# Hash attention and maxout feed-forward on one core: weight and load order, DMA transposes of x, and V sums on Pool

## The chip, the cores and the metric

The kernel runs on one core of a Trainium2 chip. The metric is the device time of one execution in microseconds (us). Five runs of the kernel before took 276.6 to 278.73 us, median 277.15.

Five engines work side by side, each through its own instructions in a fixed order: PE (TensorE: matmuls, and transposes as matmuls with an identity), ACT (ScalarE), DVE (VectorE), POOL (GpSimd) and SP (SyncE, which here issues DMAs). POOL also issues DMAs, in a queue of its own. An instruction that waits holds up all that stand behind it on its engine.

## The reference

```
q_bits = (q @ proj > 0);  k_bits = (k @ proj > 0)      # 6 bits per row
bucket = sum(bits * 2**i)
mask   = q_bucket[:, None] == k_bucket[None, :]
scores = where(mask, q @ k.T / sqrt(64), -1e9)
attn   = exp(scores - max);  attn = attn / (sum(attn) + 1e-9)
x      = (attn @ v), heads side by side                 # 3072 x 512
h      = maximum(maximum(x @ w1, x @ w2), x @ w3)       # 3072 x 768
out    = h @ w_out                                      # 3072 x 512
```

There are 4 batches of 8 heads, 768 rows each, 64 columns a head. Inputs and output are float32; the matrix products run in float16 pieces.

## The kernel before

**Attention.** Heads are worked in pairs, so a batch has pairs 0 to 3, written (b, pr). For each pair q and k are loaded (`load`, L236) and split into a float16 value and its remainder (`split_h` L252/L254, `split_r` L259, tile `s`), then transposed to `T`: in batches 0 and 1 by PE (`pe_T` L278, tile `tps`) and an evacuation on DVE or ACT, in batches 2 and 3 by a DMA transpose on SP (L268). `hash_mm` (L295, L297) multiplies `T` by the projections; DVE turns signs into bits, PE transposes these (`bit_T` L324), and they go to DRAM and back (`bit_out` L334 as `dr<-bt`, `bit_in` L337 as `T<-dr`), since they must lie in other partitions of `T`: these are the hash rows. With them one score matmul gives product and bucket match together. For pair (0, 0) the rows come by PE instead.

A *unit* is one head's 384 query rows against 256 keys: two score matmuls `sc` (L380), one exponential `AT` (L386, 128x768 on ACT) and six matmuls `av` (L398) with V and a column of ones. There are 192 units, in blocks of six; a block fills the only `av` bank, which `norm_t` (L415) and `norm_x` (L421, L433) empty into `xn`. A *half* (b, hf) is 384 rows of a batch with all heads. Batch 0 runs pair 0 for both halves first, then pairs 1 to 3 of half 0, then of half 1; later batches run half by half.

**Mean of V.** `norm_t` adds a tiny multiple of the column sums of V. `vcast` (L188, L190) casts V to float16 (`vone`; on POOL in batch 0, on ACT later). In batch 0 `mean_mm` (L358) sums with six matmuls a pair from `vone`; in later batches `vsum` (L348 to L351) adds the six chunks on POOL in three instructions, and `mean_mm` (L361) is one matmul. `mean_evac` (L367) takes the result `svp` to `mv`.

**Feed-forward.** Each half needs x transposed (`xT`): `x_T` (L448, tile `xps`, three PE transposes a pair) with `x_evac` for both halves of batch 0 and for the last half, `x_bar` (L441), one DMA transpose on SP, for the other five. Then come 18 groups of four `ps` matmuls (`l1`, L462) with evacuation and maximum (L471), and three groups of six `po` matmuls (`l2`, L476), copied out (`osb`) and stored (L485). The weights are loaded on POOL's queue with a cast to float16: six loads (three matrices, left and right half; L519) and `w_out` (L634). `weights` ties groups of these loads to hash rows by `hold` (L624), a tiny POOL copy that waits for the rows.

**Order.** A planner (`Plan.run`, L44) sets the order of every engine at build time. Each task has an engine or a choice of two, an assumed duration, a priority (mostly its unit number), and the buffers it takes and gives; the planner steps through assumed time and emits the ready task of lowest priority for each free engine. Transfers run in its model as rings, and `POST` is the assumed time from a transfer's end to its notice. The instructions then run in this order whatever the real times are. Loads of batch 1 and later are tied by `after` to hash rows having been issued (`g`, L544).

Of the kernel before, what the change touches and what calls it, by code (L numbers as in the profile page):

```python
# [13 lines left out]

POST = 2.0

# [10 lines left out]
class Plan:  # L27
# [16 lines left out]
    def run(self):  # L44
# [8 lines left out]
        busy = dict.fromkeys(engines, 0.0)  # L53
        rings = {e: [] for e in engines}
        now, events, n = 0.0, [], 0
        while n < len(self.tasks):
            moved = True
            while moved:
                moved = False
                for e in engines:  # L60
                    if busy[e] > now:
                        continue
                    best = None
                    for t in ready:
                        dur = dict(t.kinds).get(e)
                        if dur is None or any(self.free[r] <= 0 for r in t.take) or any(
                                x.start is None for x in t.after):
                            continue
                        if best is None or (t.prio, t.n) < (best[0].prio, best[0].n):
                            best = t, dur  # L70
                    if best is None:
                        continue
                    t, dur = best
                    ready.discard(t)
                    for r in t.take:
                        self.free[r] -= 1
                    busy[e] = now + dur
                    t.start, t.engine = now, e
                    events.append((busy[e], -1, None))
                    if t.xfer:  # L80
                        events.append((busy[e] + 0.9, -2, t))
                    else:
                        events.append((now + dur + (t.lat or self.LAT[e]), t.n, t))
                    if t.emit:
                        t.emit(e)
                    n += 1
                    moved = True
            events.sort(key=lambda x: x[:2])
            heads = [r[0] for r in rings.values() if r]
            after = min((h[0] for h in heads)) * len(heads) if heads else 1e9  # L90
            if not events and not heads:
                stuck = [(t.kinds, t.prio, [r for r in t.take if self.free[r] <= 0])
                         for t in sorted(ready, key=lambda t: t.prio)]
                raise RuntimeError(f"plan stuck: {n} of {len(self.tasks)} at {now}, {self.free}: {stuck[:12]}")
            then = min(now + after, events[0][0] if events else 1e9)
            for h in heads:
                h[0] -= (then - now) / len(heads)
            now = then
            for r in rings.values():
                while r and r[0][0] < 1e-6:  # L100
                    t = r.pop(0)[1]
                    events.append((now + POST, t.n, t))
            events.sort(key=lambda x: x[:2])
            while events and events[0][0] <= now:
                at, kind, t = events.pop(0)
                if kind == -2:
                    rings[t.engine].append([t.xfer, t])
                    continue
                if t is None:
                    continue  # L110
                for r in t.give:
                    self.free[r] += 1
                for x in users.get(t, ()):
                    left[x] -= 1
                    if not left[x]:
                        ready.add(x)
# [4 lines left out]
def kernel(  # L121
# [37 lines left out]
    HT = 13  # L159
    XN = 3  # L160
    OSB = 3
# [47 lines left out]
    PAB = konst.tile([P, 2 * NBITS], FP16, name="PAB")  # L209
    xn0 = konst.tile([P, 2, CH, P], FP16, name="xn0")  # L210
    w_sb = [konst.tile([P, NJ, DF], FP16, name=f"w{i}_sb") for i in range(3)]
# [141 lines left out]
    def mean_mm(b, pr, e):  # L353
        ps = bank(("m", b, pr), "svp")
        o = ps[:, 0 : 2 * (D + 1)].rearrange("p (h d) -> p h d", h=2)
        if b == 0:
            for c in range(NCH):
# [59 lines left out]
    def norm_x(blk, e):  # L417
# [4 lines left out]
        if items[0][0] == items[1][0]:  # L422
            hf = items[0][0]
            if (b, hf) not in xhs:
                xhs[b, hf] = xnp.tile([P, NP, CH, P], FP16, tag="xn", name="xn")
            xn = xns[b, hf, pr] = xhs[b, hf][:, pr]
            xv = xn.rearrange("p c (h d) -> p h c d", h=2)
        else:
            hh = items[0][1]
            xv = xn0[:, :, :, hh * D : (hh + 1) * D]  # L430
            for hf in range(2):
                xns[b, hf, pr] = xn0[:, hf]
        nc.vector.tensor_tensor(out=xv, in0=t[:, :, :, 0:D], in1=rr[:].to_broadcast([P, 2, CH, D]), op=AluOp.mult)  # L433
# [6 lines left out]
    def x_bar(b, hf, e):  # L440
        nc.sync.dma_start_transpose(x_tile(b, hf)[:].rearrange("p j (c t) -> p (j c) t", t=P),  # L441
                                    xhs.pop((b, hf))[:].rearrange("p j c d -> p (j c d)"))

# [81 lines left out]
    def value(b, pr, dep):  # L525
        U = first_unit[b, pr]
        prev = at_last.get((b - 2, pr))
        if b == 0:
            ready_v[b, pr] = add(("POOL", 0.85), U - 6, [dep, prev], lambda e: vcast(b, pr, e), give=("v",))
            vs = ready_v[b, pr]  # L530
        else:
            ready_v[b, pr] = add(("ACT", 0.72), U - 6, [dep, prev], lambda e: vcast(b, pr, e))
            vs = add(("POOL", 2.0), U - 5, [dep, ready_v[b, pr], ready_m.get((b if pr > 1 else b - 1, (pr + 2) % 4))],
                     lambda e: vsum(b, pr, e), give=("v",))
        m = add(("PE", 0.34 if b == 0 else 0.06), U - 3, [vs], lambda e: mean_mm(b, pr, e), take=("mm",))
        ready_m[b, pr] = add(("DVE", 0.28), U - 3, [m], lambda e: mean_evac(b, pr, e), give=("mm",))

    def prep(b, pr):
# [3 lines left out]
        if b > 0:  # L542
            for n in "qkv":
                g = {("q", 0): (0, 1), ("k", 0): (0, 2), ("v", 0): (0, 2)}.get((n, pr), (0, 3) if pr < 2 else (1, 0)  # L544
                                                                            ) if b == 1 else divmod(4 * b + pr - GATE, 4)
                loads[n, b, pr, (0, 2)] = add(("SP", 0.5), U - 44 + 0.1 * "qkv".index(n), [],
# [59 lines left out]
        if b == 0 and pr < NP - 1:  # L606
            return_later.append(pr)
            for hh in range(2):
                ready_T[b, pr, hh] = [bi]
            return  # L610
        if (b, pr) == (0, NP - 1):
            weights(0, 0, [(0, 0), (0, 1)])
            for i in return_later:
                weights(0, i, stage[0, i])
        if (b, pr) in stage:
# [10 lines left out]
    def weights(b, pr, parts):  # L626
        if pr or b:
            prev = add(("POOL", 0.1), -150, [bounced[b, pr]], lambda e: hold(b, pr, e), after=[wprev[0]])
        else:
            prev = ready_v[0, NP - 1]  # L630
        for w in parts:
            if w == "o":
                prev = add(("POOL", 0.8), -90, [],
                           lambda e: nc.gpsimd.dma_start(wout_sb[:], moe_w_out.rearrange("(c p) m -> p c m", p=P)),  # L634
                           xfer=4.2, after=[prev])
            else:
                prev = add(("POOL", 0.8), -100, [], lambda e, w=w: load_w(w[1], w[0], e), xfer=1.9, after=[prev])
            wload[w] = prev
        wprev[0] = prev

    wprev = [None]
    return_later = []
    stage = {(0, 1): [(0, 2)], (0, 2): [(1, 0)], (0, 3): [(1, 1), (1, 2)], (1, 0): ["o"]}

# [25 lines left out]
    u = 0  # L670
    done_x, starts, has_xn = {}, {}, {}
    prev_norm = None
    for blk, (b, pr, items) in enumerate(blocks):
# [16 lines left out]
        if blk == last_block[b, pr]:  # L690
            at_last[b, pr] = prev_at
        nt = add(("DVE", 0.56), u - 20, [prev_at, ready_m[b, pr]], lambda e, blk=blk: norm_t(blk, e), take=("t",), give=("av",))
        split = items[0][0] != items[1][0]
        hf = items[0][0]
        nx = add(("DVE", 0.76), u - 20, [nt], lambda e, blk=blk: norm_x(blk, e), give=("t",),
                 take=() if split or (b, hf) in has_xn else ("xn",), after=[] if split else has_xn.get((b, hf), []))
        if split and blk == 0:
            prev_norm = nx
            continue
        if not split:  # L700
            has_xn.setdefault((b, hf), [nx])
        for hf in (0, 1) if split else (hf,):
            lst = done_x.setdefault((b, hf), [])
            tk = ("xT",) if not lst else ()
            if b == 0 or (b, hf) == (B - 1, 1):
                t = add(("PE", 0.17), u, [nx, prev_norm] if split else [nx], lambda e, b=b, hf=hf, pr=pr: x_T(b, hf, pr, e),
                        take=("mm",) + tk, after=starts.get((b, hf), []))
                starts.setdefault((b, hf), [t])
                lst.append(add(both(0.36, 0.48), u - 20, [t], lambda e, b=b, hf=hf, pr=pr: x_evac(b, hf, pr, e), give=("mm",)))
                if len(lst) == NP:  # L710
                    plan.join(lst, ("xn",))
            else:
                lst.append(nx)
                if len(lst) == NP:
                    lst = [add(("SP", 1.4), u, lst, lambda e, b=b, hf=hf: x_bar(b, hf, e), xfer=2.1, take=("xT",), give=("xn",))]
                    ffn(b, hf, lst)
                continue
            if len(lst) == NP:
                ffn(b, hf, lst)
# [32 lines left out]
```

## Time and profile before

| What | Value |
|---|---|
| median of five runs | 277.15 us |
| the profiled execution | 275.96 us |
| its span, first to last instruction | 274.2 us |
| exponentials on ACT, 192 | 146.6 us busy, 813 ns each |
| `ps` on PE, 576 | 105.2 us busy |
| `sc` on PE, 384 | 94.0 us busy |
| `av` on PE, 1152 | 66.4 us busy |
| `po` on PE, 144 | 33.7 us busy |
| `xps` on PE, 36 | 3.8 us busy |
| `svp` on PE, 24 and 12 | 2.2 and 2.6 us busy |
| first score, first `ps`, last unit done | 13.3, 52.2, about 214 us |

The span of the profile is shorter than the time of that execution by what lies outside the first and last instruction. A group's busy time is the union of its instructions; [...]bars overlap and the step from start to start is shorter than the bar. Idle time in brackets in a timeline is what the engine stood before that instruction, with the one that ended it.

### The profile page before, as it was taken

Reading aid. Unit: us, or ns where it says so; the run is one execution under the profiler, and the core shown is the slowest. Engines: PE = TensorE matmul, PEld = TensorE weight load, DVE = VectorE, ACT = ScalarE, POOL = GpSimd, SP = SyncE. Lnnn points to the kernel's source line nnn. Section 1 sums busy time; section 2 is a strip of 40 time slices with the busy share of each in tenths; the row PEclk is TensorE's granted clock in tenths of the full one; section 3 lists DMA queues with packets and bytes.
Section 4 is the critical chain, followed back from the end, with each engine's and each line's share of the span. In section 5 each row is a group of like instructions: output and inputs, shape, how many; then the busy total and the mean of one; then the engine's idle time right before and its main releaser. Section 6 shows DMA issues by size and latency. Waiting matters only on the chain.

```text
span 274.2 us, 7528 instructions
## 1 busy us (share of the span) xinstructions
PE 264.1 (96%) x3086; PEld 180.8 (66%) x3086; DVE 178.6 (65%) x400; ACT 200.0 (73%) x290; POOL 39.7 (14%) x57
## 2 busy tenths in 40 slices
PE   8899888999999999999999999999999999999994
PEld 7889666777766676676666666666666556555551
DVE  4899558999997578795499834565436635345260
ACT  4797689999996889999789888999886232322322
POOL 1250314553411103330033000000000000000000
PEclk9799799999999999999999999999999999999998
DMA  6949699795569896998969622300430021020303
GB/s 200 365 132 176 152 258 146 250 224 186 183 119 256 183 285 173 228 207 188 238 203 215 131 73 93 54 2 13 47 118 0 2 77 39 24 93 0 115 2 115
DMA packets 57872, 38.16 MB, mean 139 GB/s; under 512 B 38638, under 2 KB 54766, under 8 KB 57838
## 3 DMA queue, kind: packets, MB, share of 16 engines
q1 hardware_dynamic: 53806, 34.54, 49.1%
q0 software_dynamic: 3952, 3.15, 8.0%
q8 instruction: 24, 0.39, 0.6%
q14 instruction: 10, 0.08, 0.1%
q10 hardware_dynamic: 80, 0.00, 0.0%
HBM read 25.72 MB, written 6.84 MB: 119 GB/s over the span
## 4 chain that ended last, share of the span: by engine, by line
PE 79%; DVE 8%; DMA 6%; ACT 4%; issue 1%; SPq 1%; ACTq 0%; DVEq 0%
PE ps L462 31%; PE sc L380 19%; PE po L476 11%; PE av L398 11%; DMA k<-in_k_dram 4%; PE tps L278 3%; DVE s L259 3%; PE hps L297 2%; ACT AT L386 2%; DMA dr<-bt 2%; DVE ht L471 1%; DVE T L190 1%; DVE xn L433 1%; DVE t L415 1%; ACT vone L188 0%
## 5 line engine op out<-in xcount | busy, mean ns | idle before, releaser
L386 ACT ACTIVATE AT<-sc 128x768 f16<-128x768 f32 x192 | 146.6, 813 | 14.7 <-PE sc L380 13.9
L462 PE MATMUL ps<-xT,w_sb 128*128 128x384 f16 x576 | 105.2, 326 | 0.4 <-DVE ht L471 0.2
L380 PE MATMUL sc<-T 128*128 128x384 f16 x384 | 94.0, 328 | 2.1 <-ACT AT L386 1.7
L471 DVE TENSOR_TENSOR ht<-ht,ps 128x384 f16<-128x384 f16 x96 | 53.0, 552 | 38.0 <-PE ps L462 34.4
L398 PEld LDWEIGHTS <-AT 128*128 128x128 f16 x1152 | 60.5, 98 | 23.9 <-issue 0.9
L462 PEld LDWEIGHTS <-w_sb 128*128 128x128 f16 x576 | 52.8, 98 | 30.9 <-issue 1.0
L398 PE MATMUL av<-vone,AT 128*128 128x65 f16 x1152 | 66.4, 193 | 0.0
L188 ACT CAST ht<-ps 128x384 f16<-128x384 f32 x32 | 15.3, 479 | 33.0 <-DVE ht L471 25.5
L380 PEld LDWEIGHTS <-T 128*128 128x128 f16 x384 | 30.5, 98 | 12.9 <-issue 2.8
L476 PE MATMUL po<-wout_sb,ht 128*128 128x512 f16 x144 | 33.7, 379 | 0.0
L415 DVE TENSOR_TENSOR t<-av,mv 128x390 f32<-128x390 f32 x32 | 17.9, 560 | 14.5 <-PE av L398 14.4
L188 ACT COPY osb<-po 128x512 f32<-128x512 f32 x22 | 12.9, 586 | 16.2 <-PE po L476 16.0
L348 POOL TENSOR_TENSOR vt<-v 128x384 f32<-128x384 f32 x12 | 13.8, 1153 | 70.0 <-DMA v<-in_v_dram 69.8
L476 PEld LDWEIGHTS <-ht 128*128 128x128 f16 x144 | 13.5, 98 | 14.0
L278 PE MATMUL tps<-iden,s 128*128 128x128 f16 x216 | 19.0, 240 | 2.7 <-DVE s L259 1.7
L259 DVE SCALAR_TENSOR_TENSOR s<-q,s 128x384 f16<-128x384 f32 x32 | 20.3, 651 | 1.5 <-ACT s L252 1.4
L433 DVE TENSOR_TENSOR xn<-t,rr 128x384 f16<-128x384 f32 x32 | 20.2, 631 | 1.1
L259 DVE SCALAR_TENSOR_TENSOR s<-k,s 128x384 f16<-128x384 f32 x32 | 19.0, 610 | 0.8 <-ACT s L252 0.8
L278 PEld LDWEIGHTS <-s 128*128 128x128 f16 x216 | 15.1, 108 | 4.5 <-DVE s L259 3.8
L190 DVE CAST ht<-ps 128x384 f16<-128x384 f32 x16 | 8.9, 555 | 12.5 <-PE ps L462 12.3
L190 DVE COPY T<-tps 128x768 f16<-128x768 f16 x27 | 14.7, 552 | 2.8 <-PE tps L278 2.4
L188 ACT CAST vone<-v 128x768 f16<-128x768 f32 x12 | 10.1, 838 | 0.0
(52 smaller groups left out, 145.8 us busy)
## 6 DMA issues: line engine op xcount, KB each, us to landing
v<-in_v_dram SPq DMA_DIRECT2D x16, 384.0 KB
out_dram<-osb SPq DMA_DIRECT2D x24, 256.0 KB
q<-in_q_dram SPq DMA_DIRECT2D x15, 384.0 KB
k<-in_k_dram SPq DMA_DIRECT2D x15, 384.0 KB
w_sb<-in_moe_w_dram POOLq DMA_DIRECT2D x6, 384.0 KB, 6.6
wout_sb<-in_moe_w_out_dram POOLq DMA_DIRECT2D x1, 768.0 KB, 11.5
dr<-bt SPq DMA_DIRECT2D x15, 36.0 KB
T<-dr SPq DMA_DIRECT2D x15, 36.0 KB
```

The source lines that it names most:

```text
L188: nc.scalar.copy(o, i)
L190: ENG[e].tensor_copy(o, i)
L259: nc.vector.scalar_tensor_tensor(out=s[:, a0:a1, D : 2 * D], in0=raw_view(n, b, pr, heads), scalar=QS, in1=s[:, a0:a1, 0:D], op0=AluOp.mul ...
L278: nc.tensor.transpose(p16[:, c * P : (c + 1) * P], S16[b, pr][:, a0 + c, :], iden[:])
L380: nc.tensor.matmul(sc[:, i, 0:HQ], t[:, NA2 + hh * NCH + 2 * j + i, :], t[:, hh * NCH + hf * CH : hh * NCH + (hf + 1) * CH, :], start=True ...
L386: nc.scalar.activation(AT[:], scs.pop(u)[:, :, 0:HQ], ActFn.Exp, bias=EXP_BIAS, scale=EXP_SCALE)
L398: nc.tensor.matmul(av[:, o : o + D + 1], AT[:, i, c * P : (c + 1) * P], vones[b % 2][:, 2 * pr + hh, 2 * j + i, 0 : D + 1], start=slot == ...
L415: nc.vector.tensor_tensor(out=t[:, :, :, 0 : D + 1], in0=av[:, :, :, 0 : D + 1], in1=mv, op=AluOp.add)
L433: nc.vector.tensor_tensor(out=xv, in0=t[:, :, :, 0:D], in1=rr[:].to_broadcast([P, 2, CH, D]), op=AluOp.mult)
L462: nc.tensor.matmul(ps[:, 0:HQ], w_sb[i][:, jc, fb * P : (fb + 1) * P], xTs[b, hf][:, jc, :], start=jc == 0, stop=jc == NJ - 1)
L471: nc.vector.tensor_tensor(out=ht[:], in0=ht[:], in1=ps[:, 0:HQ], op=AluOp.max)
L476: nc.tensor.matmul(ps[:], hts[b, hf, fb][:, c * P : (c + 1) * P], wout_sb[:, fb, :], start=fb == 0, stop=fb == NF - 1)
```

## The change

- Planner's model of transfers: one queue for all instead of a ring for each engine, 2.4 us from a POOL issue to the transfer and 0.3 from an SP issue (both 0.9 before), `POST` 1.2 instead of 2.0, and larger assumed transfers of weights.
- Weights: the three left halves are issued behind the cast of v(0, 1), with no tie to hash rows. `w(1,0)` follows the rows of (0, 3), `w(1,1)` and `w(1,2)` those of (1, 0), `w_out` those of (1, 1).
- Loads of batch 1: other ties to hash rows, so that q and k of (1, 0) come behind the rows of (0, 2), and v of (1, 0) and q, k, v of (1, 1) behind those of (0, 3).
- x: every half but (0, 0) goes by `x_bar`. For batch 0 both halves have their place in `xn0`; the pool `xn` has two buffers instead of three.
- V of batch 0: pairs 1 to 3 get `vsum` on POOL and one `mean_mm` matmul.

As every assumed time feeds the planner, the order of all engines moves. In the new order SP issues copies out of (0, 1) and (0, 2), copies in of both, q and k of (1, 0), then out and in of (0, 3); the remaining loads follow. POOL runs: casts of v(0,0) and v(0,1), three weight loads, sum of pair 1, casts of pairs 2 and 3, sums of pairs 2 and 3, `hold`. The first `ps` stands behind unit 36 (behind 37 before). In PE's order the means of pairs 2 and 3 stand just before `hash_mm` of (0, 3) and unit 12. The split of (1, 0) is on DVE for q and k (q on ACT before); ACT has nine T copies up to the first `ps` instead of four, and one split instead of three.

```diff
-POST = 2.0
+POST = 1.2
+PRE_DMA = {"POOL": 2.4}
...
                     if t.xfer:
-                        events.append((busy[e] + 0.9, -2, t))
+                        events.append((busy[e] + PRE_DMA.get(e, 0.3), -2, t))
...
-            heads = [r[0] for r in rings.values() if r]
-            after = min((h[0] for h in heads)) * len(heads) if heads else 1e9
...
+            then = min(now + queue[0][0] if queue else 1e9, events[0][0] if events else 1e9)
+            if queue:
+                queue[0][0] -= then - now
...
-    XN = 3
+    XN = 2
...
-    xn0 = konst.tile([P, 2, CH, P], FP16, name="xn0")
+    xn0 = konst.tile([P, 2, NP, CH, P], FP16, name="xn0")
...
-        if b == 0:
+        if (b, pr) == (0, 0):
             for c in range(NCH):
                 nc.tensor.matmul(o, ones[:], vones[0][:, 2 * pr : 2 * pr + 2, c, 0 : D + 1],
...
-                xhs[b, hf] = xnp.tile([P, NP, CH, P], FP16, tag="xn", name="xn")
+                xhs[b, hf] = xnp.tile([P, NP, CH, P], FP16, tag="xn", name="xn")[:] if b else xn0[:, hf]
...
         if b == 0:
-            ready_v[b, pr] = add(("POOL", 0.85), U - 6, [dep, prev], lambda e: vcast(b, pr, e), give=("v",))
-            vs = ready_v[b, pr]
+            ready_v[b, pr] = add(("POOL", 0.85), U - 6, [dep, prev], lambda e: vcast(b, pr, e), give=() if pr else ("v",))
+            vs = ready_v[b, pr] if pr == 0 else add(("POOL", 2.3), U - 5, [dep, ready_v[b, pr]] + (
+                [ready_m[0, 1]] if pr == 3 else []), lambda e: vsum(b, pr, e), give=("v",))
...
-                g = {("q", 0): (0, 1), ("k", 0): (0, 2), ("v", 0): (0, 2)}.get((n, pr), (0, 3) if pr < 2 else (1, 0)
-                                                                            ) if b == 1 else divmod(4 * b + pr - GATE, 4)
+                g = divmod(4 * b + pr - GATE, 4)
+                if b == 1:
+                    g = {("q", 0): (0, 2), ("k", 0): (0, 2), ("q", 2): (1, 0), ("k", 2): (1, 0), ("v", 2): (1, 0)}.get(
+                        (n, pr), (0, 3) if pr < 2 else (1, 1))
...
-            weights(0, 0, [(0, 0), (0, 1)])
-            for i in return_later:
-                weights(0, i, stage[0, i])
+            weights(0, 0, [(0, 0), (0, 1), (0, 2)])
...
-            prev = ready_v[0, NP - 1]
+            prev = ready_v[0, 1]
...
-    stage = {(0, 1): [(0, 2)], (0, 2): [(1, 0)], (0, 3): [(1, 1), (1, 2)], (1, 0): ["o"]}
+    stage = {(0, 3): [(1, 0)], (1, 0): [(1, 1), (1, 2)], (1, 1): ["o"]}
...
-            if b == 0 or (b, hf) == (B - 1, 1):
-                t = add(("PE", 0.17), u, [nx, prev_norm] if split else [nx], lambda e, b=b, hf=hf, pr=pr: x_T(b, hf, pr, e),
-                        take=("mm",) + tk, after=starts.get((b, hf), []))
+            deps = [nx, prev_norm] if split else [nx]
+            if (b, hf) == (0, 0):
+                t = add(("PE", 0.17), u, deps, lambda e, b=b, hf=hf, pr=pr: x_T(b, hf, pr, e),
+                        take=("mm",) + (() if lst else ("xT",)), after=starts.get((b, hf), []))
...
+            if pr == NP - 1:
+                if (b, hf) != (0, 0):
+                    lst = [add(("SP", 1.4), u, lst, lambda e, b=b, hf=hf: x_bar(b, hf, e), xfer=2.1, take=("xT",),
+                               give=("xn",) if b else ())]
                 ffn(b, hf, lst)
```

## The prediction

> **What bounds the kernel now.** I read the page's busy shares and slices first, then the windows view by stage, then the chain of waits, then the timeline before the first feed-forward matmul.
>
> ```profile
> PE 264.1 (96%) x3086; PEld 180.8 (66%) x3086; DVE 178.6 (65%) x400; ACT 200.0 (73%) x290; POOL 39.7 (14%) x57
> ...
> PEclk9799799999999999999999999999999999999998
> ```
>
> ```profile
> 13.30:28.00 14.70, 14.70 (x331) 13.15 (x329) 13.61 (x33) 11.71 (x16) 3.88 (x5) 1.00 0.72 158
> 28.00:52.20 24.20, 21.17 (x312) 15.98 (x309) 16.30 (x40) 21.10 (x30) 7.30 (x13) 0.93 0.86 192
> 52.20:214.00 161.80, 161.22 (x1996) 110.17 (x1994) 116.48 (x258) 141.50 (x199) 26.74 (x33) 1.00 0.66 150
> ```
>
> ```profile
> 224.99 11.70 PE ps L462 x72
> 236.69 3.88 PE po L476 x18
> ```
>
> The reader is to see: PE is busy nearly always, and from 52.2 us on without a break; the end (chain of waits) is a train of `ps` and `po` matmuls, after attention is over at 214. Feed-forward work is the filler: whatever PE doesn't do before 214 is added behind. So every us of PE work removed, and every us that PE doesn't stand still, comes off the end. The columns of the windows are length, then busy PE, PEld, DVE, ACT and POOL, then PE's clock, the DMA share and GB/s.
>
> Busy time hides standing still, because a matmul's bar (326 ns for 384 columns) is longer than the step to the next (11.70/72 = 0.162 us). So I count by start-to-start steps, read from the timeline: `ps` and `sc` 0.162, `po` 0.216, `av` 0.029, `tps`, `xps` and `bps` 0.056, `hps` 0.025, `svp` 0.058, the opening `wps` 0.107. Times the counts: 93.3+62.2+31.1+33.4+12.1+2.0+1.7+12.0+2.1+3.4 = 253.3 us of PE work. PE's first start is 1.1, its end 270.5, and evacuation and store of the last tile take 3.7. So 16 us of the 270.5 are waits (half-clock time among them). Where? Up to the first `ps` at 52.24 the counts give 39.8 us of work, so 12.5 us of waits; after it 213.6 us of work and 4.6 of waits.
>
> ```profile
> 24.10 0.40 SPq L236 DMA_DIRECT2D q<-in_q_dram  x1
> ...
> 24.60 0.38 SPq L334 DMA_DIRECT2D dr<-bt  x1
> ...
> 28.73 0.84 ACT L252 ACTIVATE s<-q 128x768 f16<-128x768 f32 x1 [2.44 <-DMA q<-in_q_dram]
> 28.96 0.26 SPq L337 DMA_DIRECT2D T<-dr  x1
> ...
> 29.27 0.39 SPq L236 DMA_DIRECT2D k<-in_k_dram  x1
> ...
> 36.76 0.56 DVE L254 TENSOR_SCALAR s<-k 128x768 f16<-128x768 f32 x1 [3.48 <-DMA k<-in_k_dram]
> ```
>
> These timeline rows name the waits. The rows of batch 1 are split too early in ACT's and DVE's fixed orders: ACT stands 2.44 us before q(1,0) and DVE 3.48 before k(1,0), with exponentials and evacuations queued behind. k(1,0) was issued only at 29.27, behind a hash-row copy on SP that took 24.60 to 28.96, and took 7.46 us beside two weight loads.
>
> **What the skill says.** "DMA: Bandwidth & Descriptors", "Anatomy of one DMA", gives a fixed cost of about 2 us, mostly completion. Here a quiet hash-row copy (66.67, next issue 68.28) took 1.6 us and those beside weights 4.1 and 4.4 (19.70 to 23.77, 24.60 to 28.96). "GPSIMD Engine Reference", "1. Specifications", says that Pool shares its SBUF interface with VectorE and contends with VectorE instructions that have two SBUF inputs. The trace agrees: `s<-k` at 17.02 and 18.05 took 0.89 and 0.95 us under a Pool cast, against 0.55 free, while `T<-tps`, which reads PSUM, kept 0.55. "TensorE: Matmul & The Clock Gate", "What's actually happening", ties a half clock to idle windows of about 3.4 us; the clock row has two such dips before 52 us (0.67 in 10 to 15, 0.66 in 30 to 35), each after a stretch with PE waits.
>
> **The change part by part.**
>
> 1. *Means of pairs 1 to 3.* Each was six `svp` matmuls and becomes one: 15 fewer, 15 x 0.058 = 0.9 us of PE. Added on Pool: three sums of three instructions, 2.5 us each (1.02+0.45+0.87 and gaps, from 41.84 to 44.34), 3.1 with DVE in the way (54.58 to 57.65). All fall between about 16 and 27 us.
>
> 2. *x by DMA for the second half of batch 0 and the last half.* 24 fewer `xps`, 24 x 0.056 = 1.3 us of PE, and 8 evacuations off DVE and ACT (0.27 to 0.36 each), which don't bound that stretch. Added: two transposes of `xT`, 1.4 to 3.0 us of SP each. For the last half it lies under some 56 us of feed-forward backlog, costs nothing, and the wait at 214.03 (0.36 us, `ps` after the last `xps`) goes. That of batch 0 stands in SP's queue between the copies out and in of the hash rows of (1,2). It waits for the norm after unit 47 (a unit is two score matmuls and one exponential), about 65 us; the rows would be there near 71, and unit 60, which needs them, comes near 75. Nothing, with some 4 us of cover; without it each us late is a us of PE.
>
> 3. *xn and xn0.* xn goes from 3 to 2 buffers, but batch 0 no longer uses it. A half is attended in 24 units (over 20 us) and freed by one transpose: nothing.
>
> 4. *Weights and loads moved.* Pool issues three weight loads behind the cast of v(0,1), at about 14 instead of from 18.5; on Pool they go ahead of the casts of pairs 2 and 3 (three issues of 0.8 us). The initial loads are nearly through (the 16 engines are at 1.06 share in 10 to 15, 0.24 in 15 to 20), so I take no loss there; at most v(0,3), waited for until 17.70, slips by the 2 to 3 us that one weight takes, which Pool can take as long as the mean of pair 3, just ahead of unit 12, is in time (see the slower rival). The first `ps` stays right behind the last transpose of half (0,0), so earlier weights give nothing by themselves: x came last in before too. What counts is what no longer meets: SP's order becomes out(1), out(2), in(1), in(2), then q and k of (1,0), then out(3), in(3), and (1,0) is split later on DVE and not on ACT. Out(2) then goes near 24.6 into a quiet queue: in(1) at 25, in(2) at 26.5, q and k at 27, landing near 30 instead of 28.7 and 36.8.
>
> The gain of 4 is a change of the start of the first `ps`. Up to it ACT is the pacemaker. Before: 35 exponentials at a step of 0.707, four T copies at 0.68, three splits at 0.735, one `xT` copy 0.36, two V casts at 0.72: 31.5 us; start 13.86, four idle pieces 0.68+2.44+1.36+0.98 = 5.5, small gaps 1.0: 51.8, and the first `ps` 0.4 later. After, by its order: 34 exponentials, nine copies, one split, one `xT` copy, two casts: 24.0+6.1+0.7+0.4+1.4 = 32.7. Twelve transposes fewer stand ahead of the first score (0.7 us); I start at 13.5. With the same 1.0 and 0.4 the first `ps` comes at 48.6 plus ACT's idle time. Of that, 1.1 is PE: its work between units 0 and 12 is 14.3 us, ACT's 13.3. The DVE splits under the new Pool sums: 14 two-input DVE operations in that stretch, each 0.3 us longer when overlapped (`s<-q` under Pool averages 0.80 against 0.55, `xn` 0.85), two thirds overlapped, some 3 us; DVE then has 11.4+3 = 14.4 us of work against PE's 14.3. I take 0.5 of delay; bounds 0 and 4.8 (all at the worst 1.38). Split of (1,2) on DVE stands behind loads that again meet weights: 0 to 2.5, the size of the old waits; I take 0.5. Sum 2.1, so 50.7; bounds 49.7 (PE's 1.1 alone) and 54.1 (5.5 idle, as before).
>
> *Sum.* PE work after: 253.3 - 0.9 - 1.3 = 251.1, of which 38.6 stand ahead of the first `ps` (it comes one unit earlier). 50.7 + 212.5 + 4.2 of later waits (4.6 less the 0.36) + 3.7 = 271.1. The span was 274.2, so -3.1. The profiled execution took 275.96, 1.8 over its span; the median of the runs is 277.15, 1.2 over that. I take the 3.1 off the median: 274.0.
>
> **The rivals.**
>
> *The waits only move.* The early stretch is as long as before: first `ps` at 52.2 with less work ahead. Then 52.2+212.5+4.2+3.7 = 272.6: -1.6, 275.5. For it: DVE and PE were both nearly full from 13.3 to 28 (13.61 and 14.70 of 14.70). Against: the two named waits are about wrongly timed loads, and those loads move.
>
> *The waits go almost wholly.* First `ps` at 48.6+1.1 = 49.7 and later waits 3.0, as only 2.2 of the 4.6 are single waits above 0.15 us: 268.9, -5.3, 271.9. For it: also the second half-clock dip may go, which stretched 30 to 34. Against: Pool's sums.
>
> *Slower: Pool against DVE.* In PE's order the means of pairs 2 and 3 stand ahead of hash (0,3) and of unit 12. Pool's chain is 13.9, three issues to 16.3, sum 2.5, two casts 1.7, two sums 5.0: 25.6, or 27.2 at the slow 3.1; PE reaches the place near 26. If overlapped DVE operations take over 1.0 us on average, units 0 to 12 grow from 14.7 to 19 or more and PE waits there; with out and in of the rows behind it, the first `ps` comes at 56: 56+212.5+4.2+3.7 = 276.4, +2.2, 279.4. It decides from a first `ps` later than 55.2. Against: before, only `s<-k` averaged 1.07 under Pool, the others 0.8.
>
> **How the numbers follow.** Forecast 0.5, its own range 272.5 to 275.5; only-move 0.25; almost wholly 0.15; slower 0.1. A measurement tells 0.5% from no change, 1.4 us: below 275.8 is faster. Of the forecast 0.95 is there, of only-move 0.6, of almost-wholly all: 0.77; same 0.13; slower 0.10. The range 271.2 to 276.8 takes in the three cases at or below no change with about a microsecond of spread, and leaves out the slower one and the last part of the bound of 54.1 (277.4).
>
> **What would show it.** 12 `xps` left of 36 and 21 `svp` of 36, so 3,047 matmuls. First `ps` between 49.7 and 52. ACT's wait for q(1,0) gone, DVE's for k(1,0) under 1 us. Units 0 to 12 in 14.5 to 16 us, with `s` splits of 0.7 to 1.4 us under `vt`. After the first `ps` no PE wait over 0.5 us. The forecast is wrong if Pool's sums hold `svp` past 28 us, or if a new wait of over 1 us stands between 52 and 214, most likely for hash rows (1,2) behind the `xT` transpose.

## The result, and the profile after

| | before | after |
|---|---|---|
| median over all runs, us | 277.17 | 278.23 |
| ratio, 95% interval | | 1.0001 [0.9983, 1.0018] |
| profiled execution, its span, us | 275.96, 274.2 | 280.33, 278.5 |
| a second profiled execution of after, us | | 278.78, span 277.0 |

No change that can be told, where 274.0 was forecast. The ratio compares undisturbed runs only, while a median takes in all runs, and the profiled execution of after was one of its slower ones, so sizes below are checked against the second one (experiment 5) and given by ratios and by medians where the two differ.

The head of the page of after, to be held against that of before:

```profile
PE 263.1 (94%) x3047; PEld 179.2 (64%) x3047; DVE 181.1 (65%) x393; ACT 200.3 (72%) x289; POOL 46.5 (17%) x65
...
PEclk9688899999999999999999999999999999999999
```

There are 39 matmuls fewer, as meant. But PE is busy for 94% of a longer span: it stands still more. The windows of after, cut at the first score (13.3), unit 12 (32.8), just past the first `ps` (which starts at 55.38) and the end of attention (columns as in the prediction):

```profile
13.30:32.80 19.50, 17.72 (x327) 15.12 (x325) 16.26 (x31) 14.08 (x19) 13.22 (x15) 0.85 0.65 137
32.80:56.00 23.20, 19.90 (x312) 15.20 (x309) 19.82 (x45) 21.73 (x31) 8.63 (x13) 1.00 0.80 203
56.00:214.00 158.00, 155.12 (x1941) 105.89 (x1939) 109.73 (x242) 139.08 (x194) 23.12 (x31) 1.00 0.66 155
```

Units 0 to 12 took 14.70 us before and take 19.50 now, with Pool busy for 13.22 us of it instead of 3.88. And of the 158 us to the end of attention PE is idle for 2.9, where before it was idle for 0.6 of 161.8.

The same count as in the prediction (matmuls times their step; the rest of each stage is waiting, half-clock time among it), in us as work + waits:

| stage | before | after | after, second |
|---|---|---|---|
| to the first score | 8.0 + 5.3 | 7.3 + 5.9 | 7.3 + 4.9 |
| units 0 to 12 | 14.5 + 0.1 | 14.3 + 5.2 | 14.3 + 4.1 |
| to the first `ps` | 17.2 + 7.0 | 17.0 + 5.6 | 17.0 + 5.5 |
| from there to the last matmul | 213.6 + 4.6 | 212.5 + 6.9 | 212.5 + 7.7 |
| sum | 253.3 + 17.0 | 251.1 + 23.6 | 251.1 + 22.2 |

The waits count from the start of the span, so they hold 1.1 us in which PE has not begun. So 2.2 us of work left and 5 to 7 us of waiting came: about 4 to 5 in units 0 to 12, 2.3 to 3.1 after the first `ps`, with 1.4 to 1.5 won between. Where do these come from? The timeline of after, DVE, POOL and the PE waits between 17 and 24.5 us:

```profile
17.30 1.02 POOL L346 TENSOR_TENSOR vt<-v 128x384 f32<-128x384 f32 x1
17.50 1.25 DVE L252 TENSOR_SCALAR s<-k 128x768 f16<-128x768 f32 x1
...
18.67 0.54 DVE L188 COPY T<-tps 128x768 f16<-128x768 f16 x1
...
19.95 2.25 POOL L188 CAST vone<-v 128x768 f16<-128x768 f32 x2
20.34 1.17 DVE L252 TENSOR_SCALAR s<-q 128x768 f16<-128x768 f32 x1
21.43 0.29 DVE L303 TENSOR_SCALAR bit<-hps 128x144 f16<-128x144 f32 x1
21.65 2.22 DVE L257 SCALAR_TENSOR_TENSOR s<-q,s 128x384 f16<-128x384 f32 x2
...
22.16 1.29 POOL L346 TENSOR_TENSOR vt<-v 128x384 f32<-128x384 f32 x1
...
23.80 0.28 DVE L327 TENSOR_SCALAR bt<-bps 72x256 f16<-72x256 f16 x1
...
24.13 0.23 PE L359 MATMUL svp<-vsum,ones 128*128 128x130 f16 x1 [1.20 <-DVE bt L327]
```

Read DVE downwards. A split that takes 0.55 us alone takes 1.17 to 1.25 under Pool's work, and the pair of `s<-q,s` 2.22. The copy out of PSUM between them keeps 0.54. The hash bits `bt` stand behind the splits in DVE's fixed order, and PE, at the mean that stands ahead of its next hash and scores, waits 1.20 us. The bracket names `bt`, not the sum `vsum`: what PE waits for here is DVE, not Pool.

A wait of the second kind, later, from the timeline of after between 109 and 120 us:

```profile
111.31 0.41 SPq L234 DMA_DIRECT2D v<-in_v_dram  x1
...
117.39 0.83 ACT L186 CAST vone<-v 128x768 f16<-128x768 f32 x1 [2.16 <-DMA v<-in_v_dram]
...
118.98 0.48 PE L378 MATMUL sc<-T 128*128 128x384 f16 x2 [1.46 <-ACT AT L384]
```

A load issued at 111.31 is there at 117.39, 6.1 us later; ACT's order has its cast 2.16 us too early, the exponentials behind it are late, and PE waits 1.46 us for one.

### The profile page after: what moved, and what is told of

Same layout as the page of the kernel before. It is cut to its first block, busy times and chain, and to the rows that moved or that the text cites. A ratio compares the mean times of both kernels' runs of the same rounds, so it can differ in the third digit from the quotient of the medians.

```text
span 278.5 us, 7456 instructions
## 1 busy us (share of the span) xinstructions
PE 263.1 (94%) x3047; PEld 179.2 (64%) x3047; DVE 181.1 (65%) x393; ACT 200.3 (72%) x289; POOL 46.5 (17%) x65
## 4 chain that ended last, share of the span: by engine, by line
PE 77%; DMA 8%; ACT 5%; DVE 5%; issue 2%; SPq 1%; POOL 1%; ACTq 0%; DVEq 0%; POOLq 0%
PE ps L461 31%; PE sc L378 18%; PE po L475 11%; PE av L396 10%; DMA v<-in_v_dram 5%; ACT AT L384 4%; DMA q<-in_q_dram 4%; PE tps L276 3%; DVE s L257 3%; PE hps L295 2%; PE hps L293 1%; DVE s L252 1%; SPq L234 1%; DVE T L188 1%; PE bps L322 0%
## 5 line engine op out<-in xcount | busy, mean ns | idle before, releaser
L384 ACT ACTIVATE AT<-sc 128x768 f16<-128x768 f32 x192 | 146.4, 813 | 15.3 <-PE sc L378 13.9
L470 DVE TENSOR_TENSOR ht<-ht,ps 128x384 f16<-128x384 f16 x96 | 53.1, 553 | 39.4 <-PE ps L461 36.2
L346 POOL TENSOR_TENSOR vt<-v 128x384 f32<-128x384 f32 x15 | 16.7, 1112 | 67.6 <-DMA v<-in_v_dram 67.5
L413 DVE TENSOR_TENSOR t<-av,mv 128x390 f32<-128x390 f32 x32 | 17.9, 560 | 14.8 <-PE av L396 14.7
L186 ACT COPY osb<-po 128x512 f32<-128x512 f32 x24 | 14.1, 586 | 16.5 <-PE po L475 16.3
L276 PE MATMUL tps<-iden,s 128*128 128x128 f16 x216 | 19.8, 241 | 3.3 <-DVE bit L305 1.5
L257 DVE SCALAR_TENSOR_TENSOR s<-q,s 128x384 f16<-128x384 f32 x32 | 19.5, 623 | 4.2 <-ACT s L250 4.0
L257 DVE SCALAR_TENSOR_TENSOR s<-k,s 128x384 f16<-128x384 f32 x32 | 19.9, 636 | 0.5 <-ACT s L250 0.4
L188 DVE CAST ht<-ps 128x384 f16<-128x384 f32 x17 | 9.4, 555 | 15.8 <-PE ps L461 15.8
L186 ACT COPY T<-tps 128x768 f16<-128x768 f16 x15 | 11.9, 802 | 2.2 <-PE tps L276 2.1
L252 DVE TENSOR_SCALAR s<-k 128x768 f16<-128x768 f32 x13 | 12.4, 951 | 0.0
## 6 DMA issues: line engine op xcount, KB each, us to landing
wout_sb<-in_moe_w_out_dram POOLq DMA_DIRECT2D x1, 768.0 KB, 11.6
```

The lines of the kernel that those rows point to most:

```text
L186: nc.scalar.copy(o, i)
L257: nc.vector.scalar_tensor_tensor(out=s[:, a0:a1, D : 2 * D], in0=raw_view(n, b, pr, heads), scalar=QS, in1=s[:, a0:a1, 0:D], op0=AluOp.mul ...
L276: nc.tensor.transpose(p16[:, c * P : (c + 1) * P], S16[b, pr][:, a0 + c, :], iden[:])
L346: nc.gpsimd.tensor_tensor(out=t[:], in0=v32[:, :, 0:half], in1=v32[:, :, half : 2 * half], op=AluOp.add)
L384: nc.scalar.activation(AT[:], scs.pop(u)[:, :, 0:HQ], ActFn.Exp, bias=EXP_BIAS, scale=EXP_SCALE)
L413: nc.vector.tensor_tensor(out=t[:, :, :, 0 : D + 1], in0=av[:, :, :, 0 : D + 1], in1=mv, op=AluOp.add)
```

## The experiments

Theories: (A) Pool's sums slow DVE; (B) PE waits for the sums themselves; (C) the planner's new assumed times set consumers of loads too early in the fixed orders; (D) loads and x bring what was forecast and A and C give it back; (E) they bring nothing. "Order kept" means that only what a task emits was changed, so that the planner and every engine's order stay. Medians are in us, with that of before on the same chip beside them.

**1, 3. The changed kernel without the sums,** order kept (1), or planned anew without them (3). The common edit:

```diff
     def vsum(b, pr, e):
         v32 = raws.pop(("v", b, pr))
+        if b == 0:
+            return
...
-        if (b, pr) == (0, 0):
+        if b == 0:
             for c in range(NCH):
```

> The changed kernel in its own order, but the V sums of pairs 1 to 3 of batch 0 aren't made on Pool: their means are six matmuls each again, at the same places. Theory A (Pool's sums hold up DVE's splits, and that ate the gain): units 0 to 12, 19.5 us in the changed kernel, fall to 15 to 16.5, the DVE split of k goes from 0.95 us towards 0.7, the first ps comes at 50 to 52.5 instead of 55.4, and the time is 3 us under the changed kernel although PE has 0.9 us more work: ratio to the kernel before 0.986 to 0.992. Theory B (the new order itself is slow there, with four splits on DVE that ACT made before, and weights beside the last loads): units 0 to 12 stay at 18.5 us or more, and the time rises by the 0.9 us: ratio 1.002 to 1.007.

> The changed kernel with its transfer model, weights, load ties and x by DMA, but without Pool's sums in the plan, so that the planner orders all anew. Theory A: like e1 or better, first ps before 52, ratio 0.984 to 0.992. Theory B: units 0 to 12 at 18 us or more, ratio 1.0 to 1.006.

Measured: 1: 275.4 against 277.11, 0.9945 [0.9919, 0.9971]. 3: 277.61, 0.9982 [0.9955, 1.001]. Taking the sums out with the order kept wins 2.8 us on 278.23 by the medians and 1.6 by the ratios, though it adds 0.9 us of matmuls. The ratio falls short of the 0.986 to 0.992 of theory A, and experiment 3 lies between its two theories. DVE of experiment 1, the same instructions in the same order as in the rows above from `s<-q` on (the last row, the next `s<-k`, takes 0.54 in after too):

```profile
16.72 1.18 DVE L252 TENSOR_SCALAR s<-q 128x768 f16<-128x768 f32 x1
17.82 0.29 DVE L303 TENSOR_SCALAR bit<-hps 128x144 f16<-128x144 f32 x1
18.03 1.42 DVE L257 SCALAR_TENSOR_TENSOR s<-q,s 128x384 f16<-128x384 f32 x2
19.38 0.27 DVE L327 TENSOR_SCALAR bt<-bps 72x256 f16<-72x256 f16 x1
...
20.48 0.55 DVE L252 TENSOR_SCALAR s<-k 128x768 f16<-128x768 f32 x1
```

Pool's casts still stretch one split to 1.18, but the pair takes 1.42 instead of 2.22, and PE's wait for `bt` is 0.40 instead of 1.20. Splits and normalizations in units 0 to 12 add up to 9.4 us on DVE, 11.6 with the sums. The window of that stretch in experiment 1:

```profile
11.00:27.50 16.50, 15.92 (x343) 13.84 (x341) 14.16 (x32) 14.31 (x20) 5.40 (x6) 1.00 0.87 192
```

16.50 us, with PE idle for 0.6, against 19.50 and 1.8. Most of the rest is the clock, granted in full here and 0.85 there; see the last section. Experiment 3 is the same computation in another order; its median is 2.2 us higher, though the intervals just overlap. The planner's order alone may be worth that much.

**2. Before with the sums,** order kept, means by one matmul.

```diff
     def vcast(b, pr, e):
...
+        if b == 0 and pr:
+            vsum(b, pr, e)
...
-        if b == 0:
+        if (b, pr) == (0, 0):
```

> The kernel before in its own order, with the V sums of pairs 1 to 3 of batch 0 made on Pool behind each cast and one matmul for each mean (15 matmuls fewer); the two first weight issues on Pool come some 7 us later by this. Theory A: DVE's splits in units 0 to 12 take 0.8 to 1.3 us under the sums, the stretch grows from 14.7 to 17 us or more, ratio 1.004 to 1.010 in spite of 0.9 us less PE work. Theory B: the stretch stays under 15.5 us and the time falls by the PE work, ratio 0.995 to 0.999.

Measured: 276.85, 0.999 [0.9965, 1.0014]. This is what theory B expected, not A. Units 0 to 12 take 15.3 us instead of 14.7, and 0.9 us of matmuls are gone without a gain that can be told, so in this order the sums cost at most 1.3 us (the 0.9 and the upper end of the interval). In the order of before one `split_h` of that stretch is on DVE, in that of after three. That the price of Pool's sums depends on what DVE has beside them fits this; no run varied it alone.

**12. The changed kernel with sums made but not used:** order kept, means by six matmuls from `vone`, so nothing waits for a sum.

```diff
-        if (b, pr) == (0, 0):
+        if b == 0:
             for c in range(NCH):
```

> The changed kernel in its own order, Pool's sums made as in the change but not used: the means of batch 0 are six matmuls each from the cast V, as in e1. So nothing waits for a sum; only Pool's work is there. If contention on SBUF between Pool and DVE is the cost: units 0 to 12 at 18 us or more (27.5 - 11.0 = 16.5 in e1), DVE's split of q(0,3) and k near 0.9 to 1.2 us, and a median 2.5 to 4.5 us above e1's 275.4. If the wait of PE for the sums was the cost: 16 to 17 us and the time of e1.

Measured: 278.07 against 276.71, 1.0026 [0.9998, 1.0054]. As slow as the whole change, and clear of experiment 1, from which it differs by Pool's instructions alone. Its PE timeline has the same wait at the same place:

```profile
23.31 0.52 PE L356 MATMUL svp<-vone,ones 128*128 128x130 f16 x6 [1.21 <-DVE bt L327]
```

B falls: no one waits for the sums, and the cost is there. A stands, for this order.

**4. Before with x by DMA only** (with `xn` and `xn0` as in the change).

```diff
-            if b == 0 or (b, hf) == (B - 1, 1):
...
+            if (b, hf) == (0, 0):
```

> The kernel before with x by DMA for every half but the first (xn of two buffers, xn0 for both halves of batch 0) and nothing else of the change, planned anew. If the step on x holds (24 transposes fewer, 1.3 us, and the wait of 0.36 us at the last half gone, no new wait): ratio 0.992 to 0.996. If the transpose in SP's queue holds up the hash rows of (1,2) or other copies: a PE wait of over 0.5 us between 60 and 90 us, ratio 0.998 or more.

Measured: 276.25, 0.995 [0.9927, 0.9973]: 1.4 us less by the ratio, 0.9 by the medians.

**8. Before with the new places of weights and loads only,** old planner model.

```diff
-                g = {("q", 0): (0, 1), ("k", 0): (0, 2), ("v", 0): (0, 2)}.get((n, pr), (0, 3) if pr < 2 else (1, 0)
...
+                if b == 1:
+                    g = {("q", 0): (0, 2), ("k", 0): (0, 2), ("q", 2): (1, 0), ("k", 2): (1, 0), ("v", 2): (1, 0)}.get(
...
-            weights(0, 0, [(0, 0), (0, 1)])
+            weights(0, 0, [(0, 0), (0, 1), (0, 2)])
...
-            prev = ready_v[0, NP - 1]
+            prev = ready_v[0, 1]
...
-    stage = {(0, 1): [(0, 2)], (0, 2): [(1, 0)], (0, 3): [(1, 1), (1, 2)], (1, 0): ["o"]}
+    stage = {(0, 3): [(1, 0)], (1, 0): [(1, 1), (1, 2)], (1, 1): ["o"]}
```

> The kernel before with the changed order of loads and weights alone (three left halves of weights behind the cast of v(0,1), the new ties of weights and of batch 1's loads), planned with the old model. If the forecast's step on loads holds: ACT's 2.44 us for q(1,0) and DVE's 3.48 us for k(1,0) are gone or under 1 us, the first ps comes at 49.5 to 51.5 with unit 0 near 13.3, ratio 0.992 to 0.997. If the waits only move: first ps at 52 or later, ratio 0.998 to 1.003.

Measured: 274.27 against 277.01, 0.9892 [0.9855, 0.9929]. The timeline of experiment 8 answers the rows that the prediction began with:

```profile
24.57 0.29 SPq L334 DMA_DIRECT2D dr<-bt  x1
...
26.92 0.26 SPq L337 DMA_DIRECT2D T<-dr  x1
27.23 0.40 SPq L236 DMA_DIRECT2D q<-in_q_dram  x1
27.67 0.47 SPq L236 DMA_DIRECT2D k<-in_k_dram  x1
...
30.46 0.56 DVE L254 TENSOR_SCALAR s<-q 128x768 f16<-128x768 f32 x1 [0.86 <-DMA q<-in_q_dram]
```

The copy out is followed by its copy in after 2.35 us instead of 4.36, k is issued at 27.67 instead of 29.27, the wait of 2.44 us for q is 0.86, k is no longer waited for at all, and the first `ps` is at 49.1 instead of 52.2. The gain is more than was expected. E falls.

**9. Loads and x together,** old model, no sums: the edits of 8 and 4.

> The kernel before with two parts of the change, the order of loads and weights and x by DMA, planned with the old model and with the means of batch 0 as six matmuls. If the parts add up (0.989 for loads alone, 0.995 for x alone): ratio 0.982 to 0.987, the first ps at 48 to 50, 251.8 us of PE work, and the fastest version of all. If one takes the other's cover: 0.989 or more.

Measured: 273.86 against 276.95, 0.9898 [0.982, 0.9976]; lowest median of all kernels here. The 0.982 to 0.987 of parts that add up were not reached, and that it beats experiment 8 isn't shown (six runs each, medians 0.4 apart).

**6, 11. Before with the planner's new model only:** whole (6), or all of it but the shorter latencies (11).

```diff
-POST = 2.0
+POST = 1.2
+PRE_DMA = {"POOL": 2.4}
...
-                        events.append((busy[e] + 0.9, -2, t))
+                        events.append((busy[e] + PRE_DMA.get(e, 0.3), -2, t))
```

with one queue in place of the rings and larger weights in both; experiment 11 keeps `POST` 2.0 and 0.9 for SP.

> The kernel before with the changed planner's model of transfers alone (one queue, 2.4 us from a Pool issue and 0.3 from an SP issue, POST 1.2, larger weights), all ties, weights, sums and x as before. Theory D (the model assumes that SP's loads are noticed 1.4 us sooner than before, 0.3+1.2 against 0.9+2.0, so consumers are set before the data is there): new waits of ACT and DVE for q, k or v loads of over 1 us after unit 60, ratio 1.002 to 1.010. Rival: the model fits the chip better and waits fall, ratio 0.99 to 0.998.

> The kernel before with the single queue, Pool's 2.4 us and the larger weights of the new model, but the old latencies (0.9 us to an SP transfer, POST 2.0). Theory D, with the short latencies as the cause: the waits of 4 us for k(1,0) near unit 18 and for batch 2's k near unit 88 that the whole model brought go, ratio 0.997 to 1.008 instead of 1.030. If the single queue is the cause: they stay, ratio 1.02 or more.

Measured: 6: 285.44 against 277.01, 1.0302 [1.0262, 1.0341]. 11: 277.11 against 276.95, 1.0039 [1.0007, 1.0071]. Two assumed times, together 1.4 us shorter, make this kernel 7 us slower, more than was expected. The timeline of experiment 6 between 34 and 41 us, and at 109:

```profile
38.14 0.56 DVE L252 TENSOR_SCALAR s<-k 128x768 f16<-128x768 f32 x1 [4.21 <-DMA k<-in_k_dram]
...
39.35 0.82 PE L276 MATMUL tps<-iden,s 128*128 128x128 f16 x6 [4.20 <-DVE s L257]
39.98 0.83 ACT L186 CAST vone<-v 128x768 f16<-128x768 f32 x1 [4.10 <-DMA v<-in_v_dram]
...
109.40 0.56 DVE L252 TENSOR_SCALAR s<-k 128x768 f16<-128x768 f32 x1 [1.97 <-DMA k<-in_k_dram]
```

k of (1, 0), issued at 30.82, lands 7.3 us later. The planner believes it and v to be there sooner, so DVE, ACT and PE have consumers of these loads ahead of other work, and all three stand for over 4 us. Behind 38 us half clock follows (39.4 to 42.8 in the trace's clock record).

**7, 10. The change with old latencies (7), or with the old model whole (10).** The edit of 7:

```diff
-POST = 1.2
+POST = 2.0
...
-                        events.append((busy[e] + PRE_DMA.get(e, 0.3), -2, t))
+                        events.append((busy[e] + PRE_DMA.get(e, 0.9), -2, t))
```

> The changed kernel, sums included, with the assumed latencies of before in the planner (0.9 us to an SP transfer and POST 2.0; Pool's 2.4 and the single queue stay). Theory D: the V cast on ACT no longer waits over 1 us for its load after unit 60, PE's waits from unit 72 to 120 fall from 3.4 to under 2 us, ratio 0.990 to 0.996. Rival (Pool's sums are nearly the whole loss): waits after unit 72 move little and the ratio stays at 0.998 to 1.004.

> The changed kernel with the old planner's model whole (a ring for each engine, 0.9 us to a transfer, POST 2.0, smaller weights), Pool's sums included. Theory D (the model is what ate the gain): ratio 0.982 to 0.990. Theory A (Pool's sums ate it): units 0 to 12 over 17 us, ratio 0.993 to 1.0.

Measured: 7: 275.73 against 277.01, 0.997 [0.9946, 0.9993]. 10: 275.53 against 276.95, 0.9973 [0.9939, 1.0006]. Both medians are 2.5 to 2.7 below that of after, but the ratios only 0.003 (0.8 us), and their intervals touch its own. Neither reaches what the theory of the latencies expected: in 7 the cast of V still waits 1.17 us for its load at 116.69, and 10 lies where the sums were said to be the cost. Against experiment 9, experiment 10 adds only the sums: 1.7 us more by the medians, 2.1 by the ratios.

**5. The changed kernel again,** unchanged, for a second profile.

> The changed kernel unaltered, for a second trace of another execution. If what the first trace shows is the order's own: units 0 to 12 again over 17.5 us, DVE's split of k again near 0.9 us there, the first ps after 53, and the V cast on ACT near unit 96 again waits 1 to 2 us for its load; ratio 0.999 to 1.005. If it was one execution's bad luck with the half clock alone: units 0 to 12 under 16 us.

Measured: 278.67 against 277.01, 1.0018 [0.9985, 1.0051]; profiled 278.78. Same wait of 1.20 us for `bt`, at 23.56. The wait of ACT's V cast of the first profile, expected again, is 0.34 us at most; other later waits stand at other places. From its timeline:

```profile
94.48 0.76 PE L295 MATMUL hps<-PAB,T 128*128 128x12 f16 x24 [1.46 <-DMA T<-s]
...
145.93 0.84 ACT L250 ACTIVATE s<-q 128x768 f16<-128x768 f32 x1 [2.05 <-DMA q<-in_q_dram]
...
147.52 0.48 PE L378 MATMUL sc<-T 128*128 128x384 f16 x2 [1.54 <-ACT AT L384]
```

The first two are consumers of DMAs, placed too early in a fixed order; the third waits for an exponential that stands behind the second on ACT. Which of them bites changes from one execution to the next.

## Why the prediction was wrong

**Right: the work.** 3,047 matmuls, and 253.3 to 251.1 us of PE work, the 0.9 + 1.3 that was summed. The 38.6 us ahead of the first `ps`, the 212.5 behind it and the 3.7 at the end came as summed too. The miss lies in two other numbers: the first `ps` at 55.4 and 53.1 instead of 50.7, and later waits of 6.9 and 7.7 instead of 4.2.

**A slip in the sum.** 13.5 + 32.7 + 1.0 + 0.4 is 47.6, not 48.6. The prediction's own terms put the first `ps` at 49.7 and the time at 273.0, which makes the miss larger by 1 us and explains none of it. And its 12.5 us of waits up to the first `ps` hold the 1.1 us before PE's first start, which its 16 us leave out.

**A reading that tests nothing.** The quiet hash-row copy of 1.6 us is no test of the fixed cost of about 2 us beside it: the section of the Trainium skill that the prediction quotes gives that figure for DMAs issued by GpSimd, and SP issues the hash rows. Nothing in the sum rests on it.

**Right: the loads.** ACT's wait for q(1,0) and DVE's for k(1,0) go, alone (experiment 8) and in the change. Loads and x together gave 273.86, the forecast 274.0. That was the time of these two parts, not of the change, and in part luck: in the profile of experiment 9 the first `ps` came at 49.4 and the later waits were 8.2 us. In the sum x was 1.3 + 0.36 = 1.7 us; alone it brought 0.9 to 1.4. Before also had half clock from 30.4 to 33.8, up to 1.7 us of its 7.0 of waits there. Experiments 8, 9 and 10 and both profiles of after have none in that place, but neither has experiment 2 with its old loads, and experiment 7, with the new ones, has it from 29.5 to 36.3; so that the loads removed it isn't shown.

**Right: the cover of rows (1,2).** The transpose of `xT` in SP's queue delayed nothing: no PE wait over 0.4 us stands between 60 and 90.

**Wrong, a term mis-sized: "I take 0.5 of delay; bounds 0 and 4.8"** for DVE splits under Pool's sums. Experiments 1 and 12 put the cost of making the sums at 2.2 us by their ratios (0.9945 and 1.0026) and 2.7 by their medians; units 0 to 12 took 19.5 and 18.5 us where 14.5 to 16 were expected. The value lay inside the bounds. That the sums lengthen DVE's work was sized nearly right, 2.2 us (9.4 to 11.6) where some 3 were taken. But DVE was busy for 16.3 us in the stretch, not 14.4, and the working compared DVE's total with PE's (14.3) as if only the larger sum mattered. It did not follow what stands behind the stretched splits: `bt`, for which PE waits. The 0.3 us for each overlapped instruction came from means of two-input splits; the `s<-k` of one input went from 0.55 to 1.07 us, the mean of nine of them that lay at least half under Pool. "GPSIMD Engine Reference", "1. Specifications", of the Trainium skill names, besides two SBUF inputs, DVE instructions in a two-port mode as contending with Pool; that this one is in such a mode no run here shows, but it is stretched at least as much as the others.

That was the mechanism of the slower rival, with one step false: "Pool's sums hold `svp`". Those of batch 0 don't (experiment 12). The rival's marks, a first `ps` past 55.2 and 19 us for units 0 to 12, were reached in one profile of after and missed in the other (53.1 and 18.5).

**Wrong, a second term: "4.2 of later waits (4.6 less the 0.36)".** It assumed that the later order is as good as before. They were 6.9 and 7.7 us, with PE waits of 1.46 and 1.54 us: a sign that the prediction named, though not for the rows that it suspected. The planner's model, whose new times were listed with the change and priced nowhere, has a part in it: alone it cost 8.4 us, all but 1.1 of that by the shorter latencies, and with the latencies undone the later waits were 5.6 us (experiment 7). But it isn't the whole reason. With the old model they were 6.5 us in experiments 4 and 8, 6.7 in 10 and 8.2 in 9 (up to 1.7 of it half clock), so a new order brought some 2 us of later waits whichever model made it. The largest wait of experiment 9 has nothing to do with a load that was assumed too early; from its timeline:

```profile
59.41 0.18 POOL L626 COPY hold<-T 6x1 f16<-6x1 f16 x1 [9.91 <-DMA T<-dr]
...
60.75 1.01 POOL L350 TENSOR_TENSOR vt<-v 128x384 f32<-128x384 f32 x1
...
63.16 0.27 PE L363 MATMUL svp<-vsum,ones 128*128 128x130 f16 x1 [1.83 <-POOL vsum L353]
```

Pool stands at a `hold` of weights until the hash rows are there, so a V sum of batch 1, behind it in Pool's order, comes late, and PE waits 1.83 us for it.

The worst place of experiment 6, q, k and v of (1, 0), has no such waits in after, where the loads have new places; that may be why the change loses less to the model than the model costs alone.

**The account.** Four of the kernels have loads and x moved, differ only in the sums and the model, and were each planned anew:

| ratio, 95% interval; median, us | without sums | with sums |
|---|---|---|
| old model | 0.9898 [0.982, 0.9976]; 273.86 (9) | 0.9973 [0.9939, 1.0006]; 275.53 (10) |
| new model | 0.9982 [0.9955, 1.001]; 277.61 (3) | 1.0001 [0.9983, 1.0018]; 278.23 (after) |

By the ratios loads and x bring -2.8 us, and either of the other parts alone takes back more than half of it: the sums 2.1 with the old model, 0.5 with the new; the model 2.3 without sums, 0.8 with them. By the medians, each against before on its chip, the sums are 1.7 and 0.6, the model 3.6 and 2.5. So the two losses don't add up. Of these differences only that from experiment 9 to after is clear of the intervals; that the sums cost time is clear with the order kept, from experiment 1 to 12. So D holds in its total; how much of it is A and how much C isn't shown.

**Open.** How much of the cost of the sums is PE's wait for `bt` (0.8 us more than without them) and how much half clock wasn't separated. Why later waits grow in every new order isn't shown. Between experiments 1 and 3, and 8 and 9, orders differ by chance of the planner as much as by their parts, so no part's price in a new order is known to better than a microsecond or two.

## What to carry to other kernels

A change to a planner's assumed times is a change to every engine's order: before trusting it, hold each load's assumed time against its landing in the trace in the busiest stretch, since a consumer placed early stops a whole in-order engine (4.2 us on DVE in experiment 6). Before work is put on Pool, look at what DVE does at that moment and at what stands behind it on DVE, not only at Pool's spare time or DVE's total. When a change has several parts, run the parts and their combinations: here two were worth 3 us, and two others took it back without adding up.

## What was not expected of the hardware

The first 15 us differ between executions of the same instructions: the first loads land at other times, and the clock's half-speed stretches differ. After had half clock at 9.0 to 15.8 and 26.1 to 29.5 us, its second profile 8.2 to 15.0 alone, experiment 1, in the same order, none before 146.9, and experiment 8 one of 3.41 us. The same two instructions, a split that waits for its load and the six matmuls of the first mean, in the timeline of after and then in that of experiment 1:

```profile
8.51 0.84 ACT L250 ACTIVATE s<-q 128x768 f16<-128x768 f32 x1 [1.06 <-DMA q<-in_q_dram]
...
12.65 0.81 PE L356 MATMUL svp<-vone,ones 128*128 128x130 f16 x6
```

```profile
6.95 0.84 ACT L250 ACTIVATE s<-q 128x768 f16<-128x768 f32 x1 [0.46 <-DMA q<-in_q_dram]
...
10.66 0.51 PE L358 MATMUL svp<-vone,ones 128*128 128x130 f16 x6
```

The load came 1.6 us later, the clock was half in one and full in the other (0.81 against 0.51), and the first score is 2.3 us later (13.3 against 11.0). The Trainium skill's "TensorE: Matmul & The Clock Gate", "What's actually happening", calls the clock's window free-running, so that the count of slow matmuls differs between runs; the traces agree. Here a stretch was one or two windows of 3.41 us, and the runs of after spread from 274.4 to 282.2. Of the 3.0 us by which units 0 to 12 were longer in after than in experiment 1, PE's idle time makes 1.2, and 0.9 us of matmuls are fewer; so 2.7 lie in longer bars: half clock was granted in 5.9 us of the stretch in after and in none of it in experiment 1. A single pair of profiles would have put all of it down to the sums. The prediction tied half clock to idle windows of about 3.4 us; these traces show it after much shorter waits. In the 3.41 us ahead of the stretch at 26.1 in after PE stood for 1.20 us, ahead of that at 30.4 in before for 1.06; and in the second profile of after the same wait of 1.20 us was followed by none.

Pool's contention was larger than the 0.3 us taken for it on the one-input `s<-k` (0.55 us alone, 1.07 in the mean and up to 1.36 under Pool), absent on DVE instructions that read PSUM (`T<-tps` and `t<-av,mv` keep 0.54 to 0.56), and absent under Pool's issuing of DMAs (14.89 to 17.29 us of after, where a pair of splits took 1.13). Pool's own additions vary too: `vt<-v` takes 1.01 us at 109.78 and 1.39 at 24.68 in after.
